# Loading and working a second batch by halves of its heads, in a kernel whose order is written out by hand

## The chip, the cores and the metric

The kernel runs on one core of one Trainium2 chip. The metric is the device time of one execution in microseconds (us), read as the median of several runs. In the profile PE is TensorE's matmuls, PEld its weight loads, DVE is VectorE, ACT is ScalarE, POOL is GpSimd and SP is SyncE. "L265" is line 265 of the kernel as it was before the change.

## What is computed

A linear attention without softmax, normalised by its root mean square, and a channel mix behind it:

```python
kv = np.einsum('bhsd,bhse->bhde', k, v)
out = np.einsum('bhsd,bhde->bhse', q, kv)
rms = np.sqrt(np.mean(out * out, axis=-1, keepdims=True) + 1e-06)
x = out / rms * g_norm          # then heads side by side: (8, 576, 512)
xk = mu_k * x + (1.0 - mu_k) * x_prev
xr = mu_r * x + (1.0 - mu_r) * x_prev
k = np.maximum(xk @ w_k, 0.0)
v = k * k @ w_v
r = 1.0 / (1.0 + np.exp(-(xr @ w_r)))
return (r * v).astype(np.float32)
```

There are 8 batches of 8 heads, 576 positions and 64 channels per head. `x_prev` is x one position earlier, zero at the first. The inputs are fp32; w_k is 512 by 1024, w_v 1024 by 512, w_r 512 by 512. All matmuls but a small one run in bf16.

## The kernel before, in words

**Two kinds of units.** The attention goes by batch (8, numbered b). The mix goes by groups of 512 rows of the 4608 (9 groups, numbered g). Group 0 needs batch 0 only, group 1 the last 64 rows of batch 0 and most of batch 1.

**Names of the pieces.** The program first registers pieces of work, each with a name, its engine and what it depends on (`Plan.add`). Then `Plan.emit` (L41) walks the text `ORDER` (L15) word by word and issues the pieces, so each engine's queue has the order of that text. An ending such as `@A` or `@D` picks ACT or DVE for a piece that can run on either. The word `z:512` is no piece: it issues one matmul of 512 columns by zero (`zeros`, L436), which adds nothing to the sum and keeps PE occupied; the first of them is in the piece `zz`.

For a batch b, with z for a half of its heads (z is 0 or 1, four heads each) and i for a half of the positions:

- `ld.k`, `ld.v`, `ld.q`: loads by POOL's queue, which change fp32 to bf16 on the way (L217). The first half of k and v of batch 0 comes by SP's queue instead, as fp32 (`ldh`, L234), and is cast by `cst` on ACT or DVE. `ld.wk`, `ld.wv`, `ld.wr` are the weights, `small` the vectors mu and g (SP).
- `kv` (PE, L258): k times v, with 64 by 64 matmuls. `kc` copies the result out of PSUM, `ks` (PE, L268) splits it by even and odd channels, `kd` copies that. `tq` (DVE, L349) transposes q. `u` (PE, L274) is q times kv, which leaves x unscaled and transposed.
- `uc` copies u out of PSUM times g (`scale`, L132), `sq` (ACT, L370) squares it. `ss` (PE, L394 or L376) sums the squares over the channels of a head, `rs` (ACT, L286) takes the inverse root. For batches 2 to 7 `rs` holds one row per head and `sp` (SP, L413) spreads it over the partitions by eight small DMAs; batches 0 and 1 get it from `ss` already spread.
- `mul` (DVE, L391) makes x. `d` is the difference to the position before, `mk` and `mr` multiply it by the vectors, `xk` and `xr` add x (`blends`, L294). xk and xr are rings of four batches.

For a group g:

- `k` (PE; L464 for group 0, L487 for the others) is xk times w_k, eight pieces `kg.0` to `kg.7` that each sum over four blocks of 128 channels, two pieces to one PSUM tile. `relu` (ACT, L452) and `ksq` (DVE) follow. Group 0 is cut further: `k0.HIZ` is position half H, half I of the 1024 columns, head half Z.
- `r` (PE, L512) is xr times w_r, `sig` its sigmoid (ACT), `v` (PE, L533) the squares times w_v, `out` the product (DVE), `st` the store (SP).

**Buffers.** PSUM is held as four tiles of two banks (`"ps"`, L114), one of which `zz` and the zeros hold until group 0 is through. k, v and q have three buffers each, so the loads of batch b wait until batch b-3 is used up. `Buf.t` is allocated at the first `get`.

**Halves.** Batch 0 is loaded and worked by halves z: its `kv`, `ks`, `u` exist twice (`zss`, L329). Batch 1 has its loads of k and v cut in two (L244) but its q in one, and is worked in one: `kv1.01`, `ks1.01`, `u1.01.0`. Its mix group 1 starts a `k` piece when xk is there for both halves (L496).

**The text ORDER** up to the first group's end, with repeats counted:

```
ldh.v ldh.k ld.q0.0 ld.q0.1 ld.v0.1 ld.k0.1 ld.v1.0 seta zz setb setp ident perm ld.wk0 ld.k1.1 ld.wk1 ld.v1.1
ld.k1.0 ld.q1.01 ld.wv0 ld.wv1 ld.wr ... table cst.v1@D cst.v0@A cst.k0@D cst.k1@D (z:512 16 times) kv0.0 ...
```

`seta`, `setb` and `setp` clear and set constants on DVE, `ident` and `perm` are made by POOL from what `setp` clears, `table` loads ACT's function table.

Of the kernel before, what the change touches and what calls it, by code (L numbers as in the profile page):

```python
# [12 lines left out]


ORDER = """  # L15
ldh.v ldh.k ld.q0.0 ld.q0.1 ld.v0.1 ld.k0.1 ld.v1.0 seta zz setb setp ident perm ld.wk0 ld.k1.1 ld.wk1 ld.v1.1 ld.k1.0 ld.q1.01 ld.wv0 ld.wv1 ld.wr ld.k2.01 ld.v2.01 ld.q2.01 table cst.v1@D cst.v0@A cst.k0@D cst.k1@D z:512 z:512 z:512 z:512 z:512 z:512 z:512 z:512 z:512 z:512 z:512 z:512 z:512 z:512 z:512 z:512 kv0.0 kc0.0@A z:512 z:512 ks0.0 tq0.0.0 tq0.0.1 tq0.1.0 small z:512 z:512 tr9 cols kd0.0@A u0.0.1 uc0.01@A sq0.01 tq0.1.1 z:512 u0.0.0 sq0.00 z:512 z:512 z:512 z:512 z:512 z:512 z:512 kv0.1 ld.v3.01 ld.k3.01 ld.q3.01 uc0.00@D kc0.1@A ss0.01 ss0.00 rs0.01 ks0.1 mul0.01 kd0.1@A rs0.00 mul0.00 z:512 z:512 z:512 u0.1.1 uc0.11@D sq0.11 u0.1.0 sq0.10 z:512 z:512 z:512 z:512 z:512 z:512 z:512 z:512 z:512 z:512 z:512 ss0.10 uc0.10@A d0.00 mk0.00@D xk0.00 k0.000 k0.010 d0.01 mr0.01@D mk0.01@D xk0.01 ss0.11 rs0.10 mul0.10 d0.10 mr0.10@A k0.110 mk0.10@D xk0.10 k0.001 k0.011 rs0.11 mul0.11 relu0.00 d0.11 mk0.11@A xk0.11 ksq0.00 kv1.01 ld.k4.01 ld.v4.01 kc1.01@D mr0.00@D mr0.11@A relu0.01 k0.100 k0.101 relu0.10 tq1.01.1 tq1.01.0 ks1.01 kd1.01@A ksq0.01 k0.111 relu0.11 u1.01.0 uc1.10@A ksq0.10 sq1.10 uc1.00@D u1.01.1 sq1.11 ksq0.11 uc1.11@A sq1.00 v0.0.0 v0.1.0 xr0.00 xr0.10 ss1.2 sq1.01 rs1.2 ss1.3 rs1.3 v0.0.1 uc1.01@D ss1.0 v0.1.1 mul1.1 ss1.1 rs1.1 r0.0 r0.1 rs1.0 xr0.01 xr0.11 r0.2 mul1.0 d1.0 r0.3 d1.1 sig0.0 mk1.0@D xk1.0 sig0.1 out0.0 v0.2.0 v0.3.0 v0.3.1 v0.2.1 mk1.1@A xk1.1 mr1.0@A kv2.01 ld.k6.01 kc2.01@A out0.1 k1.4 ks2.01 kd2.01@A tq2.01.0 tq2.01.1 k1.5 relu1.2 u2.01.0 sq2.10 uc2.00@D sq2.00 uc2.10@D k1.2 k1.3 u2.01.1 sq2.11 uc2.01@D uc2.11@D k1.6 k1.7 mr1.1@D xr1.1 sq2.01 ss2 rs2 sp2.1 relu1.1 xr1.0 sp2.0 k1.0 k1.1 relu1.0 kv3.01 ld.k5.01 ld.q4.01 ld.v6.01 ld.v5.01 st0.1 st0.3 ksq1.1 st0.0 r1.0 r1.1 tq3.01.1 ksq1.0 r1.2 kc3.01@D relu1.3 ksq1.3 ks3.01 tq3.01.0 r1.3 kd3.01@D sig1.0 u3.01.1 uc3.01@D sig1.1 v1.3.0 v1.2.0 sq3.01 ksq1.2 sq3.11 u3.01.0 uc3.10@A uc3.11@D mul2.1 v1.3.1 v1.0.0 sq3.00 v1.0.1 sq3.10 kv4.01 ld.k7.01 ld.q6.01 ld.v7.01 ld.q5.01 d2.1 uc3.00@A ss3 v1.2.1 mul2.0 d2.0 mk2.0@D v1.1.0 v1.1.1 mk2.1@A xk2.1 kc4.01@A ks4.01 rs3 xk2.0 k2.0 kd4.01@D out1.0 out1.1 mr2.0@A xr2.0 k2.4 k2.1 mr2.1@D xr2.1 k2.6 relu2.0 k2.5 relu2.2 tq4.01.1 tq4.01.0 ld.q7.01 k2.2 ksq2.2 ksq2.0 k2.3 relu2.1 k2.7 ksq2.1 relu2.3 st0.2 r2.2 sp3.0 ksq2.3 u4.01.0 sq4.10 r2.3 sig2.1 mul3.0 v2.1.0 d3.0 v2.0.0 mk3.0@D sp3.1 mr3.0@D sq4.00 uc4.00@A mul3.1 xk3.0 v2.1.1 v2.2.0 st1.3 uc4.10@A v2.3.0 u4.01.1 sq4.11 v2.2.1 v2.0.1 d3.1 mk3.1@D v2.3.1 xk3.1 sq4.01 uc4.01@A r2.0 st1.2 uc4.11@A r2.1 mr3.1@A out2.1 k3.0 sig2.0 k3.1 out2.0 k3.2 kv5.01 relu3.0 kv6.01 xr3.1 kc5.01@D ss4 rs4 sp4.1 k3.3 ks5.01 relu3.1 kc6.01@D sp4.0 xr3.0 st2.2 ksq3.0 ksq3.1 k3.4 k3.5 r3.0 kd5.01@A relu3.2 tq6.01.0 ksq3.2 ks6.01 kd6.01@A r3.1 sig3.0 st1.0 tq6.01.1 tq5.01.0 st2.3 k3.6 k3.7 relu3.3 v3.3.0 tq5.01.1 u5.01.0 sq5.00 uc5.00@A uc5.10@A sq5.10 v3.2.0 r3.2 r3.3 sig3.1 mul4.1 u5.01.1 d4.1 sq5.01 uc5.11@A uc5.01@A ksq3.3 v3.3.1 v3.2.1 st1.1 mk4.1@D v3.0.0 xk4.1 mul4.0 d4.0 sq5.11 out3.1 v3.0.1 u6.01.0 mk4.0@D xk4.0 ss5 rs5 mr4.1@D sp5.1 mr4.0@D v3.1.0 v3.1.1 out3.0 sp5.0 sq6.00 sq6.10 k4.2 k4.3 relu4.1 k4.0 k4.1 uc6.10@D u6.01.1 xr4.0 uc6.00@A sq6.01 k4.4 k4.5 st3.2 ksq4.1 uc6.11@D uc6.01@D st3.3 sq6.11 kv7.01 kc7.01@D ss6 relu4.0 ksq4.0 relu4.2 rs6 k4.6 k4.7 relu4.3 sp6.0 xr4.1 r4.2 mul5.1 r4.3 d5.1 mk5.1@D v4.0.0 ksq4.3 ksq4.2 sig4.1 st2.1 v4.3.0 tq7.01.0 st2.0 xk5.1 v4.1.0 v4.1.1 r4.0 ks7.01 kd7.01@A mul5.0 d5.0 mr5.0@A mk5.0@D xk5.0 sp6.1 r4.1 sig4.0 tq7.01.1 mul6.0 v4.2.0 v4.2.1 v4.3.1 out4.1 st4.2 st4.3 v4.0.1 out4.0 xr5.0 k5.4 k5.5 st4.0 k5.2 relu5.2 mr5.1@A xr5.1 k5.3 relu5.1 d6.0 mr6.0@D ksq5.1 k5.0 u7.01.1 uc7.01@A uc7.11@A k5.1 k5.6 k5.7 st4.1 sq7.11 ksq5.2 relu5.0 ksq5.0 relu5.3 ksq5.3 r5.0 r5.1 v5.1.0 mul6.1 sq7.01 d6.1 mk6.1@D v5.1.1 sig5.0 xk6.1 u7.01.0 sq7.10 uc7.10@A v5.2.0 v5.0.0 v5.0.1 mk6.0@D sq7.00 uc7.00@A r5.2 r5.3 ss7 mr6.1@D xk6.0 out5.0 rs7 k6.0 sp7.0 k6.1 xr6.1 st5.0 k6.2 k6.3 xr6.0 relu6.0 k6.4 relu6.1 ksq6.0 mul7.0 k6.5 d7.0 relu6.2 mr7.0@D ksq6.2 st3.0 ksq6.1 sig5.1 sp7.1 mul7.1 d7.1 v5.3.0 v5.3.1 st5.1 xr7.0 mk7.0@D xk7.0 r6.0 r6.2 r6.3 sig6.1 r6.1 k6.6 k6.7 relu6.3 sig6.0 v6.3.0 v5.2.1 v6.2.0 st3.1 v6.1.0 ksq6.3 v6.1.1 out5.1 v6.3.1 v6.2.1 mk7.1@D xk7.1 k8.0 mr7.1@D xr7.1 k8.1 k8.2 v6.0.0 v6.0.1 out6.1 st6.2 out6.0 k8.3 relu8.1 relu8.0 k7.2 ksq8.1 st5.3 k7.4 k7.0 k7.5 relu7.2 ksq8.0 k7.3 relu7.1 ksq7.1 ksq7.2 k8.6 st5.2 st6.3 k7.6 k7.7 relu7.3 ksq7.3 k8.7 relu8.3 k7.1 relu7.0 v8.0.00 r7.0 st6.1 r7.1 sig7.0 k8.4 r7.2 r7.3 sig7.1 k8.5 relu8.2 ksq7.0 v7.3.0 v7.3.1 ksq8.3 v7.0.0 v7.2.0 v7.2.1 out7.1 st7.3 st7.2 r8.0 v7.0.1 r8.2 v7.1.0 v7.1.1 out7.0 st6.0 r8.1 sig8.0 r8.3 st7.1 st7.0 v8.2.00 sig8.1 ksq8.2 v8.0.10 out8.00 v8.1.00 v8.1.10 out8.10 st8.00 v8.2.10 out8.20 st8.10 v8.3.00 st8.20 v8.3.10 out8.30 st8.30 v8.3.01 v8.3.11 out8.31 st8.31
"""


# [12 lines left out]
class Plan:  # L32
# [3 lines left out]
    def add(self, name, on, fn, deps=(), bufs=(), also=None):  # L36
        assert name not in self.pieces, name
        p = self.pieces[name] = Piece(name, on, fn, deps, bufs, also)
        return p
# [17 lines left out]
def kernel(  # L57
# [13 lines left out]
    nc = tc.nc  # L71
# [4 lines left out]
    NHP = H // 2  # L76
# [6 lines left out]
    G = 512  # L83
# [3 lines left out]
    RING = RB * S  # L87
# [29 lines left out]
    add = plan.add  # L117

    def get(buf, dtype=None):
        if buf.t is None:  # L120
            n, shape, dt = BUFS[buf.tag]
            pool = psum if buf.tag == "ps" else sb
            buf.t = pool.tile(list(shape), dt, tag=buf.tag, name=buf.tag, bufs=n)
        return buf.t
# [24 lines left out]
    cols = const.tile([128, 9], FP32, name="cols")  # L149
# [91 lines left out]
        load_fp32(i, n)  # L241
    for b in range(B):
        for n in "kvq":
            if b < 2 and (n != "q" or b == 0):  # L244
                for z in range(NZ):
                    if b or z or n == "q":
                        load(b, n, [z])
            else:
                load(b, n, list(range(NZ)))
# [73 lines left out]
    def attention(b):  # L323
# [121 lines left out]
    def mix(g):  # L445
# [37 lines left out]
        for f2 in range(NFC // 2 if g else 0):  # L483
            ps, rt = Buf("ps"), Buf("relu")
            m = None
            for x in range(2):
                def k_mm(_, fc=2 * f2 + x, ps=ps):  # L487
                    n0 = G * g % RING
                    n1 = min(G, RING - n0)
                    for a0, a1, x0 in ((0, n1, n0), (n1, G, 0)):  # L490
                        for cc in range(NHP):
                            if a1 > a0:
                                nc.tensor.matmul(get(ps)[:, fc % 2, a0:a1], w_k_sb[:, cc, 128 * fc:128 * fc + 128],  # L493
                                                 xk[:, cc, x0:x0 + a1 - a0], start=(cc == 0), stop=(cc == NHP - 1))

                m = add(f"k{g}.{2 * f2 + x}", "T", k_mm, deps=[m] if m else need["k"] + (p_wk if g == 1 else []),  # L496
                        bufs=[ps])
                if x:
                    k_all.append(m)
            a = add(f"relu{g}.{f2}", "A", lambda _, ps=ps, rt=rt: k_relu(_, ps, rt), deps=[m], bufs=[ps, rt])  # L500

            def k_sq(_, f2=f2, rt=rt):
                nc.vector.tensor_mul(out=get(sqk)[:, 2 * f2:2 * f2 + 2, :], in0=rt.t, in1=rt.t)  # L503

            sqs[f2 // 2].append(add(f"ksq{g}.{f2}", "D", k_sq, deps=[a], bufs=[rt, sqk]))
# [98 lines left out]
```

## Time and profile before

| | us |
|---|---|
| median of 3 runs | 201.87 (201.4 to 201.99) |
| the profiled execution | 203.93 |
| its span, first to last instruction | 202.2 |
| PE busy | 190.9 |
| DVE busy | 134.3 |
| ACT busy | 125.0 |
| zero matmuls (L437), 43 of them, in PE's busy time | 12.4 |
| ACT table loads, 12 of them | 15.4 |

How to read it: a busy engine is one that has an instruction running, and PE's busy time includes the multiplications by zero. The profile's strip shows the span in 40 slices of 5.05 us, with a digit for the busy tenths of each. The chain of waits follows the last instruction back to the first, at each step to what released it. The timeline lists the instructions of an engine by start time, merged where the same line runs again at once, with the idle time before and what ended it. The DMA view gives, for each issue, the time from its start to its landing. The profiled execution took longer than the three timed runs, so sums are made against the profiled execution and then moved to the median.

### The profile page before, as it was taken

To read this page: it belongs to the slowest core of one execution; us is meant where nothing else is said; L and a number is where in the kernel's file an instruction comes from. 1 tells how busy PE (TensorE), PEld (TensorE's weight loads), DVE (VectorE), ACT (ScalarE), POOL (GpSimd) and SP (SyncE) were. 2 spreads that over 40 slices of the span, in tenths; PEclk is the share of its full clock that TensorE was granted. 3 is DMA by queue.
4 is the path that set the end of the run, shared out by engine and by line. 5 is a ranking of instruction groups with operands and counts; after the bars stand their busy time and mean duration, and the time that the engine had idled before them with its cause. 6 is when DMAs were issued, how large, how long until landed. Compare 5 with 4: busy or idle time off the path is not lost.

```text
span 202.2 us, 4282 instructions
## 1 busy us (share of the span) xinstructions
PE 190.9 (94%) x1769; PEld 93.8 (46%) x1769; DVE 134.3 (66%) x238; ACT 125.0 (62%) x163; POOL 23.3 (12%) x41
## 2 busy tenths in 40 slices
PE   7499897999999899999999999999999999999992
PEld 2145673444444344454437754444444444444451
DVE  2175877697875899767978798579577834321341
ACT  3055699796999558877996865397575206641120
POOL 7743422001141301000000000000000000000000
PEclk9999999999999999999999999999999999999999
DMA  6999999999999999994802534400162033000444
GB/s 208 213 209 207 211 203 205 216 203 212 208 234 241 273 245 264 211 217 93 259 9 58 165 83 143 174 35 3 24 197 105 0 128 134 0 0 0 156 159 156
DMA packets 21015, 30.63 MB, mean 151 GB/s; under 512 B 1916, under 2 KB 14468, under 8 KB 20996
## 3 DMA queue, kind: packets, MB, share of 16 engines
q0 software_dynamic: 11264, 16.19, 44.6%
q1 hardware_dynamic: 9588, 14.03, 22.0%
q8 instruction: 14, 0.23, 0.5%
q10 hardware_dynamic: 144, 0.13, 0.2%
q14 instruction: 5, 0.04, 0.1%
HBM read 33.56 MB, written 9.44 MB: 213 GB/s over the span
## 4 chain that ended last, share of the span: by engine, by line
PE 76%; DMA 8%; DVE 7%; ACT 6%; SPq 1%; issue 1%; DVEq 0%
PE ps L535 28%; PE ps L493 26%; PE ps L515 14%; DMA xk<-in_k_dram 4%; DMA rs<-rsc 4%; ACT relu L452 2%; PE ps L282 2%; PE ps L265 2%; PE ps L437 1%; DVE xk L313 1%; DVE md L136 1%; DVE d L300 1%; ACT md L134 1%; DVE xT L392 1%; DVE uT L136 1%; ACT rs L288 1%
## 5 line engine op out<-in xcount | busy, mean ns | idle before, releaser
L535 PE MATMUL ps<-w_v,sqk 128*128 128x512 bf16 (+1 forms) x296 | 66.3, 373 | 0.9 <-ACT sq L370 0.9
L493 PE MATMUL ps<-xk,w_k 128*128 128x512 bf16 (+1 forms) x288 | 58.9, 356 | 1.0 <-DVE xk L313 1.0
L452 ACT ACTIVATE relu<-ps 128x1024 bf16<-128x1024 f32 x36 | 35.8, 1024 | 29.9 <-PE ps L493 28.9
L535 PEld LDWEIGHTS <-sqk 128*128 128x128 bf16 x296 | 28.3, 98 | 33.8 <-issue 2.7
L493 PEld LDWEIGHTS <-w_k 128*128 128x128 bf16 x288 | 27.3, 98 | 28.0 <-issue 1.9
L515 PE MATMUL ps<-w_r,xr 128*128 128x512 bf16 x144 | 34.4, 379 | 0.0
L548 DVE TENSOR_TENSOR out<-ps,sig 128x1024 f32<-128x1024 f32 x16 | 19.5, 1223 | 21.4 <-PE ps L535 9.4
L503 DVE TENSOR_TENSOR sqk<-relu 128x1024 bf16<-128x1024 bf16 x32 | 21.3, 686 | 12.4 <-ACT relu L452 12.4
L525 ACT ACTIVATE sig<-ps 128x1024 bf16<-128x1024 f32 x18 | 18.2, 1022 | 13.4 <-PE ps L515 13.2
L370 ACT ACTIVATE sq<-ps 128x576 bf16<-128x576 f32 x32 | 19.9, 653 | 4.8 <-PE ps L282 3.0
L515 PEld LDWEIGHTS <-xr 128*128 128x128 bf16 x144 | 13.8, 98 | 15.7 <-issue 0.2
L392 DVE TENSOR_TENSOR xT<-uT,rs 128x1152 bf16<-128x1152 bf16 (+1 forms) x18 | 12.3, 685 | 7.6 <-ACT rs L288 4.3
L136 DVE TENSOR_SCALAR md<-d,cols 128x576 bf16<-128x576 bf16 (+1 forms) x52 | 15.7, 352 | 0.4
L144 ACT ACT_TABLE_LOAD x12 | 15.4, 1283 | 0.9 <-PEq L588 0.7
L134 ACT ACTIVATE uT<-ps,cols 128x576 bf16<-128x576 f32 x19 | 13.6, 744 | 1.2 <-PE ps L282 1.1
L136 DVE TENSOR_SCALAR uT<-ps,cols 128x576 bf16<-128x576 f32 x13 | 10.5, 815 | 5.2 <-ACT sq L370 3.3
L134 ACT ACTIVATE md<-d,cols 128x576 bf16<-128x576 bf16 (+1 forms) x20 | 12.7, 699 | 1.6 <-DVE d L300 1.6
L437 PE MATMUL ps<-zero 128*128 128x512 bf16 x43 | 12.4, 435 | 1.2 <-DVE zero L164 1.2
L313 DVE TENSOR_TENSOR xk<-md,xT 128x1152 bf16<-128x1152 bf16 (+1 forms) x18 | 12.3, 688 | 1.8 <-ACT md L134 1.4
L313 DVE TENSOR_TENSOR xr<-md,xT 128x1152 bf16<-128x1152 bf16 (+1 forms) x18 | 12.0, 686 | 2.1 <-ACT md L134 2.0
L349 DVE STREAM_TRANSPOSE qT<-q 128x576 f32<-128x576 f32 (+1 forms) x18 | 13.2, 761 | 0.1
L300 DVE TENSOR_TENSOR d<-xT 128x1152 bf16<-128x1152 bf16 (+1 forms) x18 | 12.4, 692 | 0.4
(49 smaller groups left out, 107.2 us busy)
## 6 DMA issues: line engine op xcount, KB each, us to landing
out_dram<-out SPq DMA_DIRECT2D x35, 256.0 KB, 3.0
q<-in_q_dram POOLq DMA_DIRECT2D x7, 576.0 KB, 19.4
k<-in_k_dram POOLq DMA_DIRECT2D x6, 576.0 KB, 17.9
v<-in_v_dram POOLq DMA_DIRECT2D x6, 576.0 KB, 21.2
rs<-rsc SPq DMA_DIRECT2D x48, 72.0 KB, 2.3
w_k<-in_moe_w_k_dram POOLq DMA_DIRECT2D x2, 512.0 KB, 12.4
w_v<-in_moe_w_v_dram POOLq DMA_DIRECT2D x2, 512.0 KB, 16.6
v<-in_v_dram POOLq DMA_DIRECT2D x3, 288.0 KB, 10.6
```

Of the source, the lines that this page charges most:

```text
L134: nc.scalar.mul(out=dst, in_=src, mul=col)
L136: nc.vector.tensor_scalar(out=dst, in0=src, scalar1=col, scalar2=None, op0=ALU.mult)
L144: nc.scalar.preload_act_table_set(name)
L313: nc.vector.tensor_tensor(out=dst[:, 2 * z:2 * z + 2, r0:r0 + w], in0=md.t[:, :, cs], in1=xT[:, :, cur], op=ALU.add)
L370: sq_ = add("sq" + name, "A", lambda _, ps=ps, sq=sq, cs=cs, w=w: nc.scalar.activation(out=get(sq)[:, :, cs], in_=ps.t[:, :, 0:w], func=AF ...
L452: nc.scalar.activation(out=get(rt), in_=ps.t, func=AF.Relu)
L493: nc.tensor.matmul(get(ps)[:, fc % 2, a0:a1], w_k_sb[:, cc, 128 * fc:128 * fc + 128], xk[:, cc, x0:x0 + a1 - a0], start=(cc == 0), stop=(c ...
L503: nc.vector.tensor_mul(out=get(sqk)[:, 2 * f2:2 * f2 + 2, :], in0=rt.t, in1=rt.t)
L515: nc.tensor.matmul(get(ps)[:, ci % 2, :], xr[:, cc, n0:n0 + 128], w_r_sb[:, cc, :], start=(cc == 0), stop=(cc == NHP - 1))
L525: nc.scalar.activation(out=get(sg), in_=ps.t, func=AF.Sigmoid)
L535: nc.tensor.matmul(get(ps)[:, bank, cs], sqk.t[:, fc, 128 * ci:128 * ci + 128], w_v_sb[:, fc, cs], start=(fc == 0), stop=(fc == NFC - 1))
L548: dv = add(f"out{g}.{c2}", "D", lambda _, ps=ps, sg=sg, ot=ot: nc.vector.tensor_mul(out=get(ot), in0=ps.t, in1=sg.t), deps=ms + [sg_done], ...
```

## The change

Five things change.

1. Batch 1's q is loaded by halves too: `ld.q1.0` and `ld.q1.1`.
2. Batch 1 is worked by halves like batch 0: `kv1.0`, `kv1.1`, and so `kc`, `ks`, `kd`, `tq` and `u` for each half. Its `ss`, `rs`, `mul` and what follows keep their sizes.
3. Each `k` piece of group 1 becomes two: first the two 128-channel blocks of half 0, then those of half 1. In a PSUM tile the order is `k1.0.0 k1.1.0 k1.0.1 k1.1.1`. The first part depends on xk of half 0 only.
4. `ORDER` is another text throughout, from the first load to the last store. Engines of pieces that can run on two are picked anew.
5. The zeros are 34 and `zz` instead of 42 and `zz`. The 16 before `kv0.0` stay.

```diff
-            if b < 2 and (n != "q" or b == 0):
+            if b < 2:
...
-        zss = [[0], [1]] if b == 0 else [[0, 1]]
+        zss = [[0], [1]] if b < 2 else [[0, 1]]
...
-            for x in range(2):
-                def k_mm(_, fc=2 * f2 + x, ps=ps):
...
-                        for cc in range(NHP):
...
-                m = add(f"k{g}.{2 * f2 + x}", "T", k_mm, deps=[m] if m else need["k"] + (p_wk if g == 1 else []),
-                        bufs=[ps])
-                if x:
-                    k_all.append(m)
+            for zs in ([[0], [1]] if g == 1 else [[0, 1]]):
+                for x in range(2):
+                    def k_mm(_, fc=2 * f2 + x, ps=ps, zs=zs):
...
+                            for cc in range(2 * zs[0], 2 * zs[-1] + 2):
...
+                    if g == 1:
+                        z = zs[0]
+                        deps = x_ready[0]["k"][2 * z:2 * z + 2] + [x_ready[1]["k"][z], p_wk[z]]
+                        deps = deps + ([m] if m else [])
+                    else:
+                        deps = [m] if m else need["k"]
+                    m = add(f"k{g}.{2 * f2 + x}" + (f".{zs[0]}" if g == 1 else ""), "T", k_mm, deps=deps, bufs=[ps])
+                    if x and zs[-1]:
+                        k_all.append(m)
```

The old `ORDER` from the first useful matmul to the first pieces of group 1's k (loads left out where "..." stands inside a line; `xN` counts repeats):

```
kv0.0 kc0.0@A z:512x2 ks0.0 tq0.0.0 tq0.0.1 tq0.1.0 small z:512x2 tr9 cols kd0.0@A u0.0.1 uc0.01@A sq0.01 tq0.1.1
z:512 u0.0.0 sq0.00 z:512x7 kv0.1 ... uc0.00@D kc0.1@A ss0.01 ss0.00 rs0.01 ks0.1 mul0.01 kd0.1@A rs0.00 mul0.00
z:512x3 u0.1.1 uc0.11@D sq0.11 u0.1.0 sq0.10 z:512x11 ss0.10 uc0.10@A d0.00 mk0.00@D xk0.00 k0.000 k0.010 d0.01
mr0.01@D mk0.01@D xk0.01 ss0.11 rs0.10 mul0.10 d0.10 mr0.10@A k0.110 mk0.10@D xk0.10 k0.001 k0.011 rs0.11 mul0.11
relu0.00 d0.11 mk0.11@A xk0.11 ksq0.00 kv1.01 ... kc1.01@D mr0.00@D mr0.11@A relu0.01 k0.100 k0.101 relu0.10
tq1.01.1 tq1.01.0 ks1.01 kd1.01@A ksq0.01 k0.111 relu0.11 u1.01.0 uc1.10@A ksq0.10 sq1.10 uc1.00@D u1.01.1 sq1.11
ksq0.11 uc1.11@A sq1.00 v0.0.0 v0.1.0 xr0.00 xr0.10 ss1.2 sq1.01 rs1.2 ss1.3 rs1.3 v0.0.1 uc1.01@D ss1.0 v0.1.1
mul1.1 ss1.1 rs1.1 r0.0 r0.1 rs1.0 xr0.01 xr0.11 r0.2 mul1.0 d1.0 r0.3 d1.1 sig0.0 mk1.0@D xk1.0 sig0.1 out0.0
v0.2.0 v0.3.0 v0.3.1 v0.2.1 mk1.1@A xk1.1 mr1.0@A kv2.01 ... kc2.01@A out0.1 k1.4 ks2.01 kd2.01@A tq2.01.0 tq2.01.1
```

The new one, from its start:

```
ldh.k ldh.v ld.q0.0 small table seta setp ident ld.v0.1 ld.k0.1 ld.q0.1 ld.q1.0 ld.v1.0 ld.k1.0 perm ld.wk0
ld.wk1 ld.k1.1 ld.v1.1 ld.wv0 ld.q1.1 ld.wv1 ld.wr ld.k2.01 ld.v2.01 ld.q2.01 zz cst.k0@A cst.k1@A cst.v1@D
cst.v0@A z:512x16 kv0.0 setb tq0.0.1 kc0.0@A z:512x2 ks0.0 tq0.0.0 tr9 kd0.0@D z:512x3 u0.0.1 sq0.01 kv0.1 ...
cols u0.0.0 sq0.00 uc0.01@D uc0.00@A kc0.1@D z:512x3 ss0.00 rs0.00 z:512 ss0.01 tq0.1.0 tq0.1.1 ... mul0.00 ks0.1
kd0.1@A d0.00 rs0.01 z:512x2 u0.1.0 uc0.10@A sq0.10 u0.1.1 uc0.11@A z:512x5 ss0.10 mul0.01 d0.01 mk0.00@D kv1.0
sq0.11 xk0.00 rs0.10 ss0.11 rs0.11 tq1.0.1 kc1.0@D ks1.0 tq1.0.0 kd1.0@A z:512x2 u1.0.0 mk0.01@D u1.0.1 sq1.00
xk0.01 k0.100 uc1.00@A uc1.01@A k0.000 sq1.01 mul0.10 d0.10 mk0.10@D xk0.10 mul0.11 d0.11 k0.010 mr0.11@A mk0.11@D
xk0.11 k0.011 relu0.01 ss1.1 rs1.1 mr0.10@D xr0.10 k0.001 k0.101 relu0.00 mr0.00@D relu0.10 kv1.1 k0.110 ss1.0
ksq0.00 ksq0.10 k0.111 kc1.1@A v0.3.0 tq1.1.0 v0.2.0 tq1.1.1 ... rs1.0 relu0.11 ks1.1 kd1.1@D ksq0.11 mr0.01@A
xr0.11 ksq0.01 xr0.00 v0.1.0 mul1.0 d1.0 u1.1.1 uc1.11@A u1.1.0 sq1.10 sq1.11 v0.0.0 xr0.01 v0.0.1 uc1.10@A v0.1.1
ss1.3 rs1.3 ss1.2 v0.3.1 rs1.2 mk1.0@D xk1.0 r0.0 mul1.1 d1.1 r0.1 sig0.0 r0.2 r0.3 sig0.1 v0.2.1 kv2.01 ...
mk1.1@D xk1.1 out0.0 k1.2.0 k1.0.0 k1.1.0 out0.1 kc2.01@D ks2.01 tq2.01.1 tq2.01.0 k1.3.0 k1.2.1 k1.3.1 mr1.0@A
kd2.01@A relu1.1 k1.0.1 u2.01.1 sq2.11 mr1.1@D k1.1.1 relu1.0 k1.6.0 k1.7.0 uc2.01@D uc2.11@D sq2.01 ksq1.1 u2.01.0
k1.6.1 k1.7.1 sq2.10 xr1.1 uc2.10@D k1.4.0 sq2.00 k1.5.0 uc2.00@D ss2 rs2 sp2.0 kv3.01 ...
```

Before group 2's first k piece the old text has all of r1 and v1, u3, ss3, kv4 and ks4; the new one has these and u4.01.0.

## The prediction

> **What bounds the kernel now.** I read the page first: engines, slices, then the chain. TensorE (PE) is busy for nearly the whole span, its digits fall only before 35 us, and DMA is full until about 90 us.
>
> ```profile
> PE 190.9 (94%) x1769; PEld 93.8 (46%) x1769; DVE 134.3 (66%) x238; ACT 125.0 (62%) x163; POOL 23.3 (12%) x41
> PE   7499897999999899999999999999999999999992
> DMA  6999999999999999994802534400162033000444
> ```
>
> Busy PE includes the multiplications by zero of L437, which compute nothing. So I read PE in order of time, in the timeline of the first 45 us. Columns: start, us from first start to last end, engine, line, what, and idle time before.
>
> ```profile
> 1.19 5.79 PE L437 MATMUL ps<-zero 128*128 128x512 bf16 x17 [1.19 <-DVE zero L164]
> 9.45 0.83 DVE L130 CAST k<-xk 128x576 bf16<-128x576 f32 x2 [4.14 <-DMA xk<-in_k_dram]
> ...
> 13.53 1.68 PE L437 MATMUL ps<-zero 128*128 128x512 bf16 x7
> 15.14 0.76 PE L265 MATMUL ps<-v,k 64*64 64x64 bf16 x36
> 17.52 0.69 PE L282 MATMUL ps<-qT,kv 32*64 32x288 bf16 x16
> 18.13 2.55 PE L437 MATMUL ps<-zero 128*128 128x512 bf16 x11
> 24.60 1.91 PE L469 MATMUL ps<-xk,w_k 128*128 128x256 bf16 x16 [0.61 <-DVE xk L313]
> 30.87 1.02 PE L282 MATMUL ps<-qT,kv 32*64 32x288 bf16 x32 [0.59 <-DVE qT L349]
> 32.74 1.89 PE L535 MATMUL ps<-w_v,sqk 128*128 128x512 bf16 x8 [0.86 <-ACT sq L370]
> 44.17 0.78 PE L265 MATMUL ps<-v,k 64*64 64x64 bf16 x72
> ```
>
> The first useful matmul starts at 9.97, once the last load by SP has landed (9.43) and been cast. From there to 44.88, where kv2.01 is done, 34.91 us pass: 26 zero matmuls take 6.31 (0.54, 0.53, 0.32, 1.61, 0.76 and 2.55), idle time 2.06 (0.61 + 0.59 + 0.86), so work takes 26.54. Later the chain of waits is one PE piece behind the other, with a single break, at k2: group 2 waits for x of batch 2, and that for the spreading of rs by DMA.
>
> ```profile
> 57.82 7.08 DMA rs<-rsc
> ...
> 65.02 0.77 DVE xT L392
> ...
> 67.84 0.76 DVE xk L313
> 68.61 0.05 issue
> 68.65 7.08 PE ps L493 x32
> ```
>
> PE had finished what stood before k2 at 67.5 (ks4.01, 67.29 + 0.22), so the break is worth 1.1. From 68.65 to 198.19 the chain holds PE alone. So a gain must come from zeros and idle time before 44.88 or from that break.
>
> **The front, up to kv2.01.** *Landings.* The software queue lands in order: v0.1 at 11.6, k0.1 at 13.0, v1.0 at 14.4 (issue plus time to landing, in the DMA view), 1.4 for each half batch; 512 KB of weights take 2.5. The new order gives q0.0 8.6, v0.1 10.1, k0.1 11.5, q0.1 12.9, q1.0 14.4, v1.0 15.8, k1.0 17.2, wk0 19.7, wk1 22.2, k1.1 23.6, v1.1 25.0, wv0 27.5, q1.1 28.9, wv1 31.4, wr 33.9 (before: 34.4). The two loads by SP change places but not bytes, so I keep 9.43; a later one would move everything. *small* costs nothing: before, SP issued it at 1.75 already. ident (0.19) ahead of v0.1 and perm (1.04) behind k1.0 on POOL are hidden: the ninth load waits for the first landing anyhow (8.90 in the timeline), and perm is ready near 7, wanted at 11.4.
>
> *First matmul.* v0 is now cast by ACT, 0.67 against 0.47 on DVE: start 10.16, **+0.2**. *setb* (1.0 of memsets, 1.09 to 2.1) now stands behind the v1 cast on DVE, and both transposes (0.75 each) and kd0.0 (0.4) queue behind it: 9.92, 10.93, 12.45, 12.86. u0.0.1 starts at 12.9 instead of 12.47. Its cover is that kv0.1 no longer waits behind zeros: 13.3, before 15.14.
>
> *Work added.* 36 matmuls of half a kv take as long as 72 of a whole (0.70 from 15.14; 0.71 from 44.17): +0.70. A ks half takes 0.34, a whole 0.22: +0.46. Eight u matmuls take 0.37, 16 of a whole 0.40: four pieces for two, +0.68. k1 keeps its matmuls. Sum **+1.84**.
>
> *Zeros taken out.* 18 instead of 26, at 0.243 (6.31 / 26): **-1.94**.
>
> *Idle.* I walked the new order with these durations, each piece starting when PE, its inputs and one of the four PSUM tiles are free (sq 0.59, uc 0.74, rs 0.74 on ACT; mul, d, xk 0.46, md 0.5 on DVE; k0 piece 0.93, v piece 0.86). ACT reading one PSUM tile keeps DVE off it, as before (1.20 idle at 14.81). The points: u0.1 done 17.65 (before 18.13), ss0.11 20.25 (0.35 idle, sq0.11 is fourth in a row on ACT), u1.0.0 22.0 (0.53 idle, kd1.0 behind two rs), k0.100 22.8, later than the 20.97 of k0.000 but with kv1.0 and u1.0 done; k0.111 done 31.5, v0.0.1 36.15, r0 39.2 to 42.7, kv2.01 done 44.3. That leaves 1.39 of idle time, **-0.67**. Bounds: no idle at all (-2.06) and half as much again as before (+1.03); I take the walk, which has every piece from a row.
>
> Together +0.2 + 1.84 - 1.94 - 0.67 = **-0.57**.
>
> **k1 by halves.** Its first halves can start without xk1.1 (42.5 in the walk), but two PSUM tiles stay open from first half to second. Walking on, u2.01.0 needs two tiles and gets them at 49.85, when relu1.0 and uc2.11 are through, PE being ready at 49.2: 0.65 lost. kv3.01 waits 0.3 for the tile of u2.00. No row of before shows this wait; its floor is nothing, its ceiling the break at k2, 1.1, twice. I take **+0.95**. rs2 then ends at 53.65, 0.43 later than before.
>
> **The break at k2.** u4.01.0 (0.4) is moved ahead of k2, so PE arrives at 67.5 - 0.57 + 0.95 + 0.4 = 68.3. rs2 to the last landing took 11.7 before (53.22 to 64.90), so now 65.4; mul, d, md and xk (0.77 + 0.77 + 0.65 + 0.76) give x at 68.3 to 68.4. The break closes: **-1.1**. After that I put nothing: no gap is there to gain, a loss of one more break of 1.1 is the bound. ACT has ten table loads instead of twelve in the new order (2.6 off a hidden engine). The end has the same last pieces and keeps its 4.0.
>
> **Sum:** -0.57 + 0.95 - 1.1 = -0.72. The profiled execution took 203.93 (span 202.2); the median of the three runs is 201.87, 2.06 lower. Set against its own time the sum gives 203.2, and against the median **201.2**.
>
> **Rivals.** (1) *PSUM is no hindrance:* relu and uc run earlier than I walk, the 0.95 vanishes: -1.67, 200.2. For it: two table loads fewer; against: ACT is the full engine there (4.99 of 5 us busy at 30 to 35). (2) *The spread of batch 2 lands late,* slower. Place: the break at k2. Loads of batches 5 and 6 are queued earlier than before, and rs<-rsc, median 2.3, took 7.08 beside such loads. From 65.4 each us of lateness is a us of PE; at 66.1 the 0.72 is used up, at 66.7 the loss is 0.6. A landing at 67.6, 2.2 late, gives +1.5: 203.4. Against: the queue was just as full before. (3) *Halves don't start earlier:* zeros out equals work in, and ACT and DVE in the front are 0.7 later than walked: 0, 201.9. (4) *The clock.* The first zeros start 0.43 apart, later ones 0.23, so the clock rises after about 4 us of work; it held through 2.99 us without work (6.98 to 9.97: two zeros at 10.74 took 0.54). That gap becomes 3.18. If the clock falls in it, about 4 us run at half rate: seven zeros 0.2 longer each, +1.4, less 0.72: 202.5. [...]
>
> **Chances.** Forecast 0.42, (1) 0.17, (2) 0.22, (3) 0.12, (4) 0.07. The measurement tells about 0.3% (0.6 us) from no change. Of the forecast 0.27 lies beyond that and 0.15 inside, of (3) 0.05 inside and 0.07 above, (2) and (4) above: faster 0.44, same 0.20, slower 0.36. The range takes in (1) with half of the front's idle time gone as well (-0.7) and (2) with a front 0.4 late: 199.5 to 203.8; it covers the front at its upper bound (202.9) and k1 at its ceiling with one later break (203.5). The forecast's own: 200.6 to 201.8.
>
> **What would show it.** First matmul at 10.2 and kv2.01 done near 44.3; 35 matmuls in L437 instead of 43; wk0 landed before k0.100 starts; idle PE before u2.01.0 and kv3.01 of 0.65 and 0.3; k2 starting at 68.3 with u4.01.0 behind it and no idle time before it; PE unbroken from there. A first landing later than 9.4, or a gap on PE behind 69 us, makes me wrong.

## The result, and the profile after

| | before | changed |
|---|---|---|
| first comparison: median (lowest to highest), us | 201.93 (201.4 to 202.21) | 200.21 (199.85 to 200.87) |
| its ratio, 95% interval | | 0.9919 [0.9899, 0.9939] |
| second comparison (run 9 below): median | 201.9 | 200.5 |
| its ratio, 95% interval | | 0.9947 [0.9925, 0.9969] |
| profiled execution, its span | 203.93, 202.2 | 200.29, 198.5 |

The changed kernel is 0.5 to 0.8% faster: 1.72 us by the medians of the first comparison, 1.07 by the ratio of the second. Ratios here leave out executions that took over 1.5% longer than the fastest one of the same kernel (beside run 9, 8 of 29 of the kernel before and 1 of 12 of the changed one).

The page of the changed kernel: engines, then PE's and DMA's busy tenths in 40 slices.

```profile
PE 189.4 (95%) x1741; PEld 94.1 (47%) x1765; DVE 136.1 (69%) x242; ACT 123.6 (62%) x161; POOL 23.8 (12%) x42
PE   7998999998997999999999999999999999999992
DMA  6999999999999999999706523242500017000064
```

PE's weak slices have moved: 5 to 10 us is full now, and the weakest between the first and the last is at 60 to 64 us (the digit 7). The timeline of PE shows what they are (start, us, line, operation, count, idle time before and what ended it).

```profile
1.19 6.44 PE L437 MATMUL ps<-zero 128*128 128x512 bf16 x17 [1.19 <-DVE ident L167]
7.56 0.76 PE L265 MATMUL ps<-v,k 64*64 64x64 bf16 x36
40.38 0.78 PE L265 MATMUL ps<-v,k 64*64 64x64 bf16 x72
62.30 0.77 PE L265 MATMUL ps<-v,k 64*64 64x64 bf16 x72 [0.85 <-DMA v<-in_v_dram]
65.45 4.85 PE L494 MATMUL ps<-xk,w_k 128*128 128x512 bf16 x21
```

The first useful matmul starts at 7.56 instead of 9.97, kv2.01 (40.38, the first L265 line of 72) is done at 41.09 instead of 44.88, and k2 (65.45) has no idle time before it. In its place kv4.01, at 62.30, waits 0.85 for a load. The chain of waits in order of time goes through that load from its issue on, and through one of k ahead of it:

```profile
19.40 17.53 DMA k<-in_k_dram
36.93 0.28 issue
37.22 24.95 DMA v<-in_v_dram
62.17 0.14 issue
62.30 0.77 PE ps L265 x72
```

Batch 4's v is issued at 37.22, when the load of k issued at 19.40 has landed, and lands itself at 62.17. In the profile before, the chain had no load behind 9.4 us.

But 2.4 of the 3.8 us won by kv2.01 are in the first matmul, and the change does not explain those. The profile of the kernel before, taken a second time (the first run below), shows them too.

### The profile page after: what moved, and what is told of

Same layout as the page of the kernel before. It is cut to its first block, busy times and chain, and to the rows that moved or that the text cites. A ratio compares the mean times of both kernels' runs of the same rounds, so it can differ in the third digit from the quotient of the medians.

```text
span 198.5 us, 4247 instructions
## 1 busy us (share of the span) xinstructions
PE 189.4 (95%) x1741; PEld 94.1 (47%) x1765; DVE 136.1 (69%) x242; ACT 123.6 (62%) x161; POOL 23.8 (12%) x42
## 4 chain that ended last, share of the span: by engine, by line
PE 66%; DMA 27%; POOL 3%; issue 1%; DVE 0%; POOLq 0%
PE ps L541 25%; PE ps L494 25%; DMA v<-in_v_dram 13%; PE ps L521 12%; DMA k<-in_k_dram 9%; DMA w_k<-in_moe_w_k_dram 6%; PE ps L282 2%; PE ps L265 1%; POOL k L226 1%; PE ps L379 1%; POOL v L226 1%; POOL q L221 1%; POOL perm L189 1%; PE ps L271 0%; DVE out L568 0%
## 5 line engine op out<-in xcount | busy, mean ns | idle before, releaser
L494 PE MATMUL ps<-xk,w_k 128*128 128x512 bf16 (+1 forms) x280 | 58.1, 355 | 0.6 <-issue 0.3
L541 PEld LDWEIGHTS <-sqk 128*128 128x128 bf16 x296 | 27.8, 98 | 32.1 <-issue 2.0
L521 PE MATMUL ps<-w_r,xr 128*128 128x512 bf16 x140 | 33.5, 379 | 0.3
L136 DVE TENSOR_SCALAR md<-d,cols 128x576 bf16<-128x576 bf16 (+1 forms) x54 | 16.4, 347 | 0.3
L349 DVE STREAM_TRANSPOSE qT<-q 128x576 f32<-128x576 f32 (+1 forms) x20 | 14.9, 762 | 2.3 <-DMA q<-in_q_dram 2.1
L134 ACT ACTIVATE md<-d,cols 128x576 bf16<-128x576 bf16 (+1 forms) x18 | 12.0, 714 | 2.7 <-DVE d L300 2.7
L437 PE MATMUL ps<-zero 128*128 128x512 bf16 x32 | 10.8, 478 | 1.7 <-DVE ident L167 1.2
```

The costliest lines, as they stand in the source:

```text
L134: nc.scalar.mul(out=dst, in_=src, mul=col)
L136: nc.vector.tensor_scalar(out=dst, in0=src, scalar1=col, scalar2=None, op0=ALU.mult)
L349: nc.vector.transpose(out=dst[part, js], in_=src[part, js])
L521: nc.tensor.matmul(get(ps)[:, ci % 2, :], xr[:, cc, n0:n0 + 128], w_r_sb[:, cc, :], start=(cc == 0), stop=(cc == NHP - 1))
L541: nc.tensor.matmul(get(ps)[:, bank, cs], sqk.t[:, fc, 128 * ci:128 * ci + 128], w_v_sb[:, fc, cs], start=(fc == 0), stop=(fc == NFC - 1))
```

## The experiments

In every diff a minus is the kernel that the sentence names and a plus the run. Times are medians; ratios are against the kernel before on the same chip.

**1. The kernel before, again.** No edit.

> The kernel before, unchanged, profiled a second time. In its first profile the second load by SP landed at 9.43 us and PE began useful work at 9.97; in the changed kernel 6.55 and 7.56. Theory L (the order of the loads sets the landing: two q loads in a row ahead of the others): again 9.2 to 9.6, first useful matmul 9.8 to 10.1. Rival C (chance: the landing varies from run to run, and the first profile, 2 us above the median, caught a late one): a landing of 6.5 to 8, first useful matmul at 7 to 8.5, span near 200.2. The time is that of before, 201.9, in both.

Median 201.56, ratio 1.0008 [0.9976, 1.0040]. Its profiled execution took 200.35, span 198.6. The DMA view of SP's second load (last number: us from issue to landing) and PE's timeline:

```profile
xk<-in_k_dram SPq DMA_DIRECT2D x1, 576.0 KB, 5.0
```

```profile
6.81 0.84 PE L265 MATMUL ps<-v,k 64*64 64x64 bf16 x36 [0.17 <-DVE k L130]
41.16 0.78 PE L265 MATMUL ps<-v,k 64*64 64x64 bf16 x72
65.06 7.08 PE L493 MATMUL ps<-xk,w_k 128*128 128x512 bf16 x32 [0.25 <-DVE xk L313]
```

The load landed 5.0 us after its issue here, at about 6.25, and at 9.43 in the first profile, with the same program. So the first landing varies from execution to execution, rival C of this run. A start 3.16 us later (9.97 against 6.81) made the first profile's span 3.6 longer: in these two executions the kernel before passes a late front on in full. The break before k2, 1.1 in the first profile, is 0.25 here (0.41 from the end of ks4.01). With this early landing a load does stand in the chain of the kernel before too: batch 2's q, issued at 22.23 and landed at 42.57, holds u2.01.0 up by some 0.2 us (44.09, 1.12 behind the start of the k1 piece ahead of it; 0.96 in the first profile).

**2. The kernel before with one load later.**

```diff
-ld.q0.0 ld.q0.1 ld.v0.1 ld.k0.1
+ld.q0.0 ld.v0.1 ld.k0.1 ld.q0.1
```

> The kernel before with one load moved: the second half of batch 0's q stands behind v0.1 and k0.1 instead of ahead of them, as in the changed kernel; all else as before. Theory L: SP's second load lands at 6.5 to 7.0 instead of 9.4, kv0.0 starts at 7.0 to 7.5; what follows moves with it as far as the zeros, v0.1 and k0.1 let it, so 0.8 to 2.0 us faster (200 to 201.1). Rival C: the landing does not depend on it, 201.9 within 0.3 us.

Median 203.97, ratio 1.0128 [1.0082, 1.0173]: neither. SP's second load landed at 6.3, but DVE's timeline, and the table by stage, show another loss. In the table the columns are the stretch, its length, the busy us of PE, PEld, DVE, ACT and POOL with counts, then granted clock, DMA share and GB/s.

```profile
11.58 0.78 DVE L349 STREAM_TRANSPOSE qT<-q 64x576 f32<-64x576 f32 x1 [2.42 <-DMA q<-in_q_dram]
```

```profile
12.00:16.00 4.00, 2.45 (x48) 1.44 (x46) 2.47 (x6) 2.93 (x5) 1.58 (x3) 1.00 1.16 208
16.00:18.00 2.00, 1.84 (x23) 0.81 (x22) 0.80 (x3) 1.11 (x2) 0.48 (x1) 0.72 1.15 213
18.00:20.00 2.00, 2.00 (x9) 0.69 (x6) 1.93 (x6) 1.40 (x3) 0.74 (x1) 0.50 1.16 206
```

The transpose of q0.1 stands early in DVE's queue, and everything behind it waited 2.42 us for that load. PE was busy only 2.45 of 4 us from 12 to 16, and the granted clock then fell to 0.72 and 0.50 between 16 and 20 us. Three of the six executions kept a clock of 1.00 and still took 203.57 to 203.83, so the wait is most of the loss and the clock the smaller part. A load can't be moved without the instructions that wait for it.

**3. The changed kernel with that load early again.**

```diff
-ld.q0.0 small table seta setp ident ld.v0.1 ld.k0.1 ld.q0.1
+ld.q0.0 ld.q0.1 small table seta setp ident ld.v0.1 ld.k0.1
```

> The changed kernel with the same load moved back: q0.1 directly behind q0.0, ahead of v0.1 and k0.1; all else as changed. Theory L: SP's second load lands at about 9.4, first useful matmul at 10.1, 1 to 2.4 us slower than the changed kernel (201.2 to 202.6). Rival C: 200.2 to 200.5.

Median 202.42, ratio 1.0014 [0.9972, 1.0055]: the whole gain is gone. The profiled execution shows little of it (200.58, span 198.8). Its SP load landed early, at about 5.9; kv0.1 waited for k0.1, which now lands one load later, and the front is 0.8 late:

```profile
11.55 0.76 PE L265 MATMUL ps<-v,k 64*64 64x64 bf16 x36 [0.61 <-DMA k<-in_k_dram]
41.16 0.78 PE L265 MATMUL ps<-v,k 64*64 64x64 bf16 x72
62.15 0.78 PE L265 MATMUL ps<-v,k 64*64 64x64 bf16 x72
```

kv2.01 starts 0.78 later than in the changed kernel, and kv4.01 still starts at 62.15, now without a wait. In this execution the 0.8 us were swallowed there, the first sign that the 0.85 at kv4.01 is slack. The twelve times fall into two parts by granted clock: six at 0.997 or more took 200.58 to 202.09, six at 0.992 or less 202.75 to 206.24. So the lost gain lies for the most part in executions whose clock fell; no profile shows one of them, and why it fell there stays open.

**4. The changed kernel with group 1's k pieces whole.**

```diff
-k1.2.0 k1.0.0 k1.1.0 ... k1.3.0 k1.2.1 k1.3.1 ... k1.0.1 ... k1.1.1
+k1.2 k1.3 ... k1.0 ... k1.1
```

> The changed kernel with group 1's k pieces whole again (each sums over all four blocks at once and waits for xk of both halves of batch 1); the eight pieces stand at every second place of the sixteen halves. In the changed kernel's profile xk1.1 was done at 39.5 and the first half piece began at 41.09, so no half piece ran ahead of it. Theory N (halves of k1 bring nothing and cost a wait for PSUM tiles: 0.35 idle before u2.01.0): 0 to 0.4 us faster, 199.8 to 200.2. Rival H (the halves are what the change lives from): 0.6 us slower or more, 200.8 and up.

Median 200.35, ratio 0.9958 [0.9927, 0.9988]: inside the interval of the changed kernel in the second comparison, a little above that of the first. The median is 0.15 above theory N's range and 0.45 below rival H's, so the halves are not what the change lives from. That whole pieces are faster, as N had it, does not show. PE before u2.01.0 in this run:

```profile
47.33 0.50 PE L282 MATMUL ps<-qT,kv 32*64 32x288 bf16 x16 [0.68 <-DVE uT L136]
```

The wait for PSUM tiles is 0.68 with whole pieces, 0.35 with halves. It belongs to the order around it, not to the halves. And the halves win nothing: xk1.1 was done at 39.50 in the changed kernel, 1.6 us before k1.2.0 began.

**5 and 6. The first landing held back in both kernels.**

```diff
+    add("dly", "D", lambda _: [nc.vector.memset(stage[:, 0], 0.0) for _ in range(1)])
-ldh.v ldh.k ... setp
+ldh.v ... setp dly ldh.k
```

(In the changed kernel the region of v, twice, and `ldh.v`.)

> The kernel before with the second load by SP held back by one memset on DVE of the region it writes, so that it is issued near 3.6 us instead of 1.24; the work is the same. Theory S (what the change gives is slack: the kernel before passes a late first landing on to its end one for one, the changed one has a wait for batch 4's v at 62 us that swallows it): useful matmuls start near 9.5 instead of 6.8, the end comes 2 us later or more, 202.5 to 204. Rival F (the change's gain is a faster front that is worth the same whatever the landing): 202.5 to 204 as well; the two differ in the next run.

> The changed kernel with its second load by SP held back in the same way (two memsets, issue near 3.9 us). Theory S: useful matmuls start 2 to 2.5 us later than in the changed kernel, kv4.01 still starts at 62 to 63 when batch 4's v lands, time 200.2 to 201.2, at most 1 us above the changed kernel. Rival F: 2 us or more above it, 202.2 to 203.

Medians 216.93 and 216.23, ratios 1.0674 [1.0632, 1.0716] and 1.0631 [1.0576, 1.0686]: far too strong to tell the theories apart. The load, issued behind four software loads, took 9.4 and 11.1 us to land; in the other profiles SP's second load took 4.6 to 6.1, and 8.2 in the first.

```profile
13.55 1.17 PE L266 MATMUL ps<-v,k 64*64 64x64 bf16 x36 [6.77 <-DVE k L130]
79.44 8.77 PE L494 MATMUL ps<-xk,w_k 128*128 128x512 bf16 x32 [3.34 <-DVE xk L314]
```

```profile
15.81 1.17 PE L266 MATMUL ps<-v,k 64*64 64x64 bf16 x36 [9.13 <-ACT v L128]
83.31 5.34 PE L495 MATMUL ps<-xk,w_k 128*128 128x512 bf16 x23 [2.24 <-DVE out L555]
```

Starts 6.7 and 8.3 us later (than in run 1 and in the changed kernel) cost the kernel before 6.7% of its time, and the changed kernel some 7% of its own (1.0631 against 0.9919 to 0.9947). PE was idle for 6.77 and 9.13 us, the granted clock fell to 0.50 from 12 us on in both, and k2 waited again later. What they show: slack does not protect the changed kernel from a delay of this size, and theory S in the form "at most 1 us" is wrong for it.

**7. Batch 4's k and v ahead of its q.**

```diff
-ld.q4.01 ld.k4.01 ld.v4.01
+ld.k4.01 ld.v4.01 ld.q4.01
-xk2.1 u4.01.0 sq4.10 st0.1 uc4.10@A k2.2 uc4.00@A sq4.00 out1.1 st1.0 mr2.0@D k2.3
+xk2.1 tq4.01.1 tq4.01.0 k2.2 out1.1 st1.0 mr2.0@D k2.3 u4.01.0 sq4.10 uc4.10@A uc4.00@A sq4.00
```

> The changed kernel with batch 4's k and v loaded ahead of its q (the transposes of that q and u4.01.0 are moved behind xk2.1 and k2.3, since q4 then lands last), and st0.1 directly behind st0.0. Theory D (the changed kernel is bound at kv4.01 by the landing of v4 at 62.2, 0.85 us of idle PE): v4 lands at 57 to 60, kv4.01 starts at 61.4 without a wait, 0.5 to 1.0 us faster than the changed kernel, 199.2 to 199.7. Rival E (the wait is only passed on, to q4 or to the spreading of batch 2's rs before k2): 200.0 to 200.4.

Median 202.16, ratio 0.9953 [0.9914, 0.9991]. The kernel before took 203.39 beside it, so only the ratio can be compared: it is that of the changed kernel to within 0.4%. No gain shows: rival E. PE and ACT:

```profile
61.10 0.78 PE L265 MATMUL ps<-v,k 64*64 64x64 bf16 x72
63.84 0.38 PE L271 MATMUL ps<-kvn,perm 128*128 128x128 bf16 x4 [1.00 <-ACT kvn L128]
```

```profile
62.79 0.74 ACT L288 ACTIVATE rsc<-ps,eps 128x576 bf16<-128x576 f32 x1 [1.34 <-DMA rs<-rsc]
63.42 0.36 ACT L128 CAST kvn<-ps 128x256 bf16<-128x256 f32 x1
```

kv4.01 no longer waits, as theory D said (the line at 61.10), but ks4.01 behind it waits 1.00 for its copy kc4.01 on ACT. That stands behind rs3, and rs3 waits 1.34 for the spreading of batch 2's rs, since there is one `rsc` buffer (L107). k2 then loses another 0.22 and 0.56; the run also moves u4.01.0 and the transposes of q4 behind it, and part of this may be theirs. Near 62 us three things end almost together: the landing of v4 (62.17 in the changed kernel's profile), the spreading of rs (62.79 here, where rs3 starts), and PE's work (61.45 in the changed kernel's profile, where kv4.01 begins to wait).

**8. The changed kernel without the 18 zero matmuls behind kv0.0.**

> The changed kernel without the 18 zero matmuls behind kv0.0 (those ahead of it stay). Theory Z (they only fill waits): the front is 0 to 0.8 us shorter, kv4.01 waits for v4 as before, 199.9 to 200.4, granted clock 1.00 throughout. Rival K (they keep the clock up): the granted clock falls below 1 between 10 and 25 us, the front gets 1 us longer or more, and the time 200.8 or more.

Median 206.48, ratio 1.0112 [1.0048, 1.0177]: rival K. Its table by stage (columns as above):

```profile
10.00:14.00 4.00, 2.55 (x57) 1.34 (x57) 2.85 (x7) 2.56 (x4) 1.53 (x3) 0.90 1.08 203
14.00:18.00 4.00, 2.64 (x33) 1.41 (x34) 3.12 (x9) 3.29 (x6) 1.73 (x3) 0.50 1.16 212
18.00:22.00 4.00, 3.48 (x58) 2.10 (x53) 3.32 (x9) 2.59 (x6) 1.05 (x2) 0.50 1.14 206
```

PE was busy 2.55 and 2.64 of 4 us, with no gap over 0.9, and the clock fell to 0.50. With the zeros the changed kernel kept it:

```profile
10.00:14.00 4.00, 3.83 (x67) 1.98 (x66) 2.77 (x7) 2.72 (x5) 1.74 (x4) 1.00 1.08 202
14.00:18.00 4.00, 3.66 (x63) 1.83 (x62) 3.83 (x11) 3.98 (x8) 1.78 (x3) 1.00 1.16 212
18.00:22.00 4.00, 3.79 (x43) 2.82 (x44) 3.83 (x11) 3.37 (x6) 0.81 (x2) 1.00 1.15 206
```

So the clock held with the zeros and fell without them: with the 18 of the new order it read 1.00 from 10 to 22 us in both profiles of the changed kernel (this one and run 9's).

**9. The changed kernel again,** beside runs 10 to 12.

> The changed kernel, unchanged, once more, as the measure for the three runs beside it. Theory G (the gain is the kernel's): 1.2 to 2 us below the kernel before of the same call, single times close together. Rival N (the kernel before only had late first landings in the first runs): within 0.6 us of it.

Median 200.5, ratio 0.9947 [0.9925, 0.9969]: between the two ranges (1.07 us, where theory G had 1.2 to 2 and rival N up to 0.6), nearer to theory G. Eleven of its twelve times lie between 199.78 and 200.73. Its profiled execution (199.78, span 197.9) had SP's second load land as early as run 1 did (the casts behind it start at 6.25, in run 1 at 6.30):

```profile
7.24 0.75 PE L265 MATMUL ps<-v,k 64*64 64x64 bf16 x36
40.39 0.78 PE L265 MATMUL ps<-v,k 64*64 64x64 bf16 x72
61.83 0.77 PE L265 MATMUL ps<-v,k 64*64 64x64 bf16 x72 [0.38 <-DMA v<-in_v_dram]
64.97 7.13 PE L494 MATMUL ps<-xk,w_k 128*128 128x512 bf16 x32
```

So the profiles of runs 1 and 9 compare the two kernels at one landing.

**10. The kernel before with the late load of run 2, and its transposes moved with it.**

```diff
-tq0.1.0 small z:512 z:512 tr9 cols kd0.0@A u0.0.1 uc0.01@A sq0.01 tq0.1.1
+small z:512 z:512 tr9 cols kd0.0@A u0.0.1 uc0.01@A sq0.01
-uc0.00@D kc0.1@A
+uc0.00@D tq0.1.0 tq0.1.1 kc0.1@A
```

> The kernel before with q0.1 loaded behind v0.1 and k0.1, and the two transposes of q0.1 moved on DVE from ahead of the copies of u0.0 to behind uc0.00, so that they no longer hold DVE up till q0.1 lands (2.42 us in the run with the load alone). Batch 1 stays whole. Theory L (the order of the first loads makes the first landing early and steady, and that is where the change's gain comes from): within 0.4 us of the changed kernel, single times close together. Rival W (the work by halves and the order behind it are what gains): 0.8 us or more above the changed kernel.

Median 202.22, ratio 1.0035 [0.9997, 1.0072], 1.7 us above the changed kernel: rival W. Its SP load landed at about 6.5 in the profile and its times still spread from 200.9 to 203.4. The later place of q0.1 among the first loads is not the gain by itself.

**11. The front of run 10 with the changed kernel's order behind kv2.01.** Batch 1 whole, k1 by halves.

> The front of the run before this one (batch 1 whole, q0.1 loaded late) up to kv2.01, and behind it the changed kernel's order with k1 by halves. Theory B (behind 44 us the changed order is pinned by the landing of batch 4's v at 62, so the front may be 0.8 us slower at no cost): within 0.3 us of the changed kernel. Rival A (the front's 0.8 us reach the end): 0.6 us or more above it.

Median 206.85, ratio 1.0274 [1.0227, 1.0320]: neither. DVE's timeline:

```profile
60.53 0.78 DVE L349 STREAM_TRANSPOSE qT<-q 128x576 f32<-128x576 f32 x1 [4.00 <-DMA q<-in_q_dram]
```

In the old front, batch 4's k and v are loaded ahead of its q. The new order transposes that q from 55 to 57 us, so DVE stood 4.00 us, and PE with it (4.09, and a granted clock of 0.94 from 40 to 70 us). The run doesn't tell the two theories apart. It shows the other side of run 7: the new back needs q4 early, and so has v4 late.

**12. A slow cast in the changed kernel.**

```diff
-copy(eng, get(kvq[(n, 0)])[:, m, :], stage[:, i, m])
+[copy(eng, get(kvq[(n, 0)])[:, m, :], stage[:, i, m]) for _ in range((4 if eng == "A" else 5) if n == "v" else 1)]
```

> The changed kernel with the casts of v0.0 repeated (ACT four times, DVE five times, the same result), so that the first useful matmul comes 1.9 us later while all loads stay where they are. Theory S (0.85 us of slack at kv4.01): kv4.01 starts about 1 us later, time 0.8 to 1.3 us above the changed kernel. Rival F (passed on in full): 1.7 us or more above; rival P (the loads bound all of it): under 0.4 us.

Ratio 1.0000 [0.9970, 1.0029] against 0.9947 for run 9 beside it: 1.06 us above the changed kernel, for a first matmul some 1.8 us later (2.83 behind the landing, where run 9 had 1.00). By the single times the interval of that difference is 0.7 to 1.4: theory S, and neither of its rivals. Of the delay some 0.8 is missing at the end. Waits for loads can have taken it in (0.38 to 0.85 at kv4.01, 0.18 to 0.52 at kv1.0, see below), but no profile shows an execution of this run that kept its clock. In four of its twelve executions the clock fell and the time was 205.8 to 211.3; its profile is one of them, with SP's load landing at about 7.3:

```profile
10.17 0.76 PE L265 MATMUL ps<-v,k 64*64 64x64 bf16 x36 [3.27 <-ACT v L128]
```

```profile
10.00:14.00 4.00, 3.83 (x55) 1.90 (x54) 2.37 (x15) 0.49 (x2) 2.01 (x3) 0.73 1.09 203
14.00:18.00 4.00, 4.00 (x58) 2.11 (x51) 2.69 (x4) 2.01 (x4) 1.50 (x2) 0.50 1.16 214
```

## Why the prediction was right, and where it was not

The side was right and the time lay in the range; the size, -0.72, was less than half of the first comparison's -1.72 and two thirds of the second's -1.07, and the narrower range, 200.6 to 201.8, was missed by 0.1 to 0.4. Set against each other at one landing (the profiles of runs 1 and 9):

| point, us | before | changed | difference |
|---|---|---|---|
| the cast behind SP's second load starts | 6.30 | 6.25 | -0.05 |
| first useful matmul | 6.81 | 7.24 | +0.43 |
| kv2.01 done | 41.87 | 41.10 | -0.77 |
| kv4.01 starts | 60.76 | 61.83, ss3 and four v matmuls (1.2) more ahead of it | -0.15 at equal work, with 0.38 of waiting |
| k2 starts | 65.06 | 64.97, u4.01.0 (0.38) ahead of it | -0.47 at equal work |
| PE's last matmul done | 194.60 | 194.14 | -0.46 |
| time | 200.35 | 199.78 | -0.57 |

- **What bounds the kernel:** zeros and idle time in front, and the break at k2, as read. What one profile could not tell is that its first landing, 9.43, was a late one. At an equal landing the forecast's sum came near (-0.57 measured, -0.72 forecast), but that is luck in part. The front came out 0.2 better than forecast, k1 0.4 cheaper and the break 0.7 smaller, the wait of 0.38 at kv4.01 was missing from the sum, and run 1 had 0.2 of waiting at u2.01.0 that the first profile did not have.
- **First matmul, +0.2:** it became +0.43, but not by the cast. The 17 zeros ahead of kv0.0 ended at about 7.2, with the cast of v0 done at 7.0 after this early landing, so they stood in the way. They took 6.11 us in run 9 and 5.46 in run 1; over all profiles they took 5.46 to 6.75, in both orders. In eight of the fourteen profiles they, and not the landing, set the first useful matmul, so most of the +0.43 belongs to these two executions.
- **The front, -0.57:** -0.77 at kv2.01. From first matmul to kv2.01 it takes 33.86 (41.10 - 7.24) instead of 35.06 (41.87 - 6.81), so work added, zeros taken out and idle time give -1.20, where the walk had 34.14 against 34.91, -0.77.
- **k1 by halves, +0.95:** 0.35 before u2.01.0, and about 0.2 at kv3.01 (49.48 instead of 49.28, where ss2 ended). The tiles were too few where the walk said, for less time, and run 4 shows that the halves are not the reason.
- **The break at k2, -1.1:** it did close, but it was worth only 0.41 at an early landing. The 1.1 belonged to the late execution.
- **"After that I put nothing":** the term that was missing stands just ahead of k2, kv4.01's wait for v4. The walk listed landings up to wr and took later loads as given, though the new order puts q4 ahead of k4 and v4, one more load of 576 KB. Such loads landed about 2.8 us apart (batch 2's three at 36.9, 39.7 and 42.4 in the changed kernel's profile), but v4 landed 4.5 to 5.2 us later than in the two profiles of the kernel before (62.17 against 57.7 and 56.9). The rest is that k4 and v4 landed 3.5 and 4.5 us behind the load ahead of each; the spreading of rs and the first stores ran at that time, but no run shows that they are the cause. Rival (2) had a late transfer too, but another one and some 3 us further on, at k2.
- **Rival (1)** had a sum of -1.67, near the first comparison's -1.72, by a way that the runs don't show: luck. **Rival (4)** did not happen in the changed kernel as profiled: useful work started at 7.56 with no idle time ahead of it, and the granted clock read 1.00 up to 22 us. Run 12 has a fall behind a gap: after 3.27 us of idle PE the clock was 0.92 from 11 to 12 us and 0.50 from 12 to 13, where it had held after 2.99 in the first profile. But it fell in run 8 too, to 0.50 with no gap over 0.9, so the runs show no length of gap that decides it. Nor do they show a clock that rises after some 4 us of work, as the rival had it: the zeros do come closer together (0.43 us apart, then 0.22), but the granted clock reads 1.00 from the start.

**What makes up the rest of the gain.** The evidence points to slack. The kernel before passes a late front on one for one (two executions, run 1 and the first profile: 3.16 at the start, 3.6 at the end). The changed kernel reaches two waits whose ends are set by the load queue and not by the front. The first is at kv1.0. Its two profiles start their useful work at 7.56 and 7.24, 0.32 apart, and are together there:

```profile
16.78 0.76 PE L265 MATMUL ps<-v,k 64*64 64x64 bf16 x36 [0.18 <-DMA k<-in_k_dram]
16.80 0.75 PE L265 MATMUL ps<-v,k 64*64 64x64 bf16 x36 [0.52 <-DMA k<-in_k_dram]
```

kv2.01 then starts at 40.38 and 40.39. The second is kv4.01's wait for v4 at 62 us. That load landed at 62.17 and 61.7 in these two profiles, at 61.5 in run 3, whose front was 0.8 late, and at 59.6 in run 12's, whose front was 5 us late. So the changed kernel gives back only 1.06 of some 1.8 (run 12).

The single times beside run 9 fit that. Those that its ratio counts lie between 199.78 and 200.73 for the changed kernel and between 200.31 and 202.29 for the one before. The lowest differ by 0.53, about the gain at equal landing; the highest by 1.56. How much of the gain each wait makes up is not measured, and run 3 can't be counted for it, since its loss lies with the clock.

**What stays open:** why the landing varies, and whether the new order of the first loads makes a late one rarer. All profiles of the changed order had it land between 5.9 and 7.3, but one profile catches one execution. Run 10 speaks against it: with q0.1 moved as in the new order its times still spread over 2.5 us at a clock of 0.995 or more. Why the time of the 17 zeros varies, and why the clock fell in half of run 3's executions, is open as well. Whether the better front would be worth more with the three waits near 62 us apart was tried once only (run 7) and did not show.

## What to carry to other kernels

Take a second profile before summing from the first: one late transfer at the start was in the first one's total, and more than half of the 1.1 at k2 came with it. When a front gets faster, list the landings of every load up to the next place where the old kernel waited, since here the load queue set the next limit: v4 landed 25.0 us after its issue, and PE waited 0.85 for it (0.38 in run 9). Such a wait took in part of an earlier delay: in run 3's profile kv2.01 started 0.78 late, and kv4.01 at 62.15 against 62.30. And move a load only together with the instructions that wait for it.

## What the hardware did that was not expected

- The same load of 576 KB, issued at the same time in the same program, landed 5.0 (run 1) and 8.2 us later (the first profile). Issued 2.4 and 2.8 us later, behind four software loads, it took 9.4 (run 5) and 11.1 (run 6).
- The 17 zeros ahead of kv0.0 start 0.43 us apart at first and 0.22 later. The change came at 4.5 us in run 1 and at 5.9 in run 9, with the same zeros, while the granted clock of the profile is 1.00 all that time.
- The clock fell after a gap of 3.27 us without work on PE (run 12) and not after one of 2.99 (the first profile). In run 12 PE had work again from 10.17 on, and the clock was still 1.00 from 10 to 11 us, 0.92 from 11 to 12 and 0.50 from 12 to 13.
- It also fell with no gap over 1.0 us, where PE had been busy 61% (run 2, 12 to 16 us) and 55% of the time (run 8, 8 to 13 us). The busy share of some 4 us does not explain it alone: in the first profile PE was busy for 1.03 us of the 4 from 7 to 11 (26%), and the clock held. Over 4 us at a time from 10 to 22 us the changed kernel was busy 83% or more in both profiles, and it held.
- Eighteen zero matmuls of some 4 us in all are worth about 1.7% of the time, 3.3 us, by ratios from two sets of runs (1.0112 and 0.9947).
